# Queries turned three steps ahead through GpSimd, the minimum first on VectorE, and four weight chunks prepared in the first layer instead of in attention

## The chip, the cores and the metric

One core of a Trainium2 chip runs the whole program. The metric is the device time in microseconds (us). The kernel before was timed three times: 667.3, 667.43 and 668.02 us, median 667.43 us.

## The reference

The input is attention with a local window and block summaries (2 batches, 8 heads, 768 positions, head size 64), followed by two gated layers on 1536 tokens (512 to 2048 to 512). Cut to what is computed:

```
k_sum = max of k over blocks of 32;  v_sum = mean of v over blocks of 32
s_l = q k^T / 8, only where |i - j| < 16;  s_s = q k_sum^T / 8 + log(32)
a = softmax([s_l, s_s]);  x = a [v; v_sum]          (heads side by side: 1536 x 512)
h = x w1_in;  x = (h cos h) w1_out                  (layer 1)
h = x w2_in;  out = (h tanh(softplus h)) w2_out     (layer 2)
```

## The kernel before, in words

**Attention** (`attention`, lines 198 to 521) works on pairs of heads: 8 pairs, each cut into 3 chunks of 256 positions, so 24 steps `i = 3n + c` (pair `n`, chunk `c`). The loop at line 507 runs a software pipeline over these steps. In iteration `i` it does the scores of step `i` (`scores`: a mask product and four 128x118 products into bank `i % 2`, a minimum over each row on VectorE, four exponentials on ScalarE with row sums; the scores are negated, so the minimum stands for the maximum), the reciprocal and scaling of step `i - 1` (`softmax`, reciprocal on VectorE, product on GpSimd), the transposes of the probabilities of step `i - 2` (`probsT`, copied to SBUF by ScalarE as `pt`), the product with the values of step `i - 3` (`pv`), and the split of the result of step `i - 4` into a high part `xh` (ScalarE) and a low part `xl` (VectorE) in `evac`.

Beside these, the table `PREP` (lines 376 to 408) says in which iteration the inputs of later pairs are loaded and prepared. `prep_k` turns 256 columns of keys with TensorE, copies them into `KX` on ScalarE and takes block maxima on VectorE; `prep_ks` spreads the maxima into gaps of `KX` on GpSimd. `prep_q` turns queries and writes them into the block-diagonal `QB`, with two 64x256 VectorE operations for each chunk, one iteration before the scores that read it. `prep_vm` makes block means of the values with 24 products, and `prep_vs` copies them into `VW` by DMAs issued from SyncE (SP); for later pairs the block sums come from GpSimd (`load_vb`, `block_sums`). There is one tile `vb`, so the second `load_vb` (planned for iteration 7) waits until GpSimd has written the sums `vs` of the first (iteration 8), and the loads planned behind it wait with it on SP's queue.

Nothing reorders the instructions: `at` collects those of one iteration by phase and `flush` emits them phase by phase in the order of `ORDER` (line 262), so each engine gets its work in exactly that order. Before the change the order on VectorE is `xl` (step `i - 4`), minimum (step `i`), reciprocal (step `i - 1`), query writes, key maxima. On ScalarE it is `xh`, `pt`, exponentials, key copy. After `flush` comes `filler(i)`, which emits what `AT` holds for iteration `i`.

**Weights** are 64-bit floats in memory. A chunk of 128x512 is loaded (`wload`), narrowed to 32 bits in four parts (`wnarrow`: one on ScalarE at line 131, three on VectorE at lines 135, 138 and 141), and split into a high part (ScalarE, line 149) and a low part (line 152, on GpSimd for the first group, else on VectorE). The first group of layer 1 has 8 chunks: chunks 0 to 3 of `w1_in`, 4 to 7 of `w1_out`. Before the change `AT` spreads all eight over iterations 1 to 23 of attention. In the layers, `WSEQ` gives the same work for later groups, by tile number.

**Layer 1** (`layers`, the loop at line 623) takes 48 tiles `k`. `up(k)` is 12 products into bank `k % 4` (2.7 us at full clock). VectorE and ScalarE then make the gate: `turns(k)` (two VectorE operations, lines 551 and 552), in the next iteration `cos_gate` (sine on ScalarE, line 558 on VectorE) and `split` (line 544). After `split` come the operations of `WSEQ[k]`. `down` is 12 products that take four tiles of gates and chunks 4 to 7 of the group, one chunk for each three products. The first `down` stands after `up(6)`. `up(0)` to `up(2)` run inside the last iterations of attention. `up(k + 4)` needs the bank that `cos_gate(k)` has read. Layer 2 has its own order and isn't touched.

Of the kernel before, what the change touches and what calls it, by code (L numbers as in the profile page):

```python
# [21 lines left out]
def kernel(  # L22
# [122 lines left out]
    def wsplit(l, g, c, part=None):  # L145
        x = wstage[l, g, c]
        hi, lo = wdst(l, g, c)
        if part != 1:
            nc.scalar.copy(hi, x)  # L149
        if part != 0:  # L150
            eng = nc.gpsimd if (l, g) == (0, 0) else nc.vector
            eng.tensor_tensor(out=lo, in0=x, in1=hi.bitcast(F32), op=ALU.subtract)
# [45 lines left out]
    def attention(filler):  # L198
        with ExitStack() as es:
# [61 lines left out]

            ORDER = ("xh", "xl", "sc", "max", "rec", "norm", "tp", "pth", "exp", "tr", "ev", "kmax", "pv", "misc")
            todo = {o: [] for o in ORDER}

# [78 lines left out]
            def prep_ks(n):  # L343

                ks = KS.pop(n)
                x = KX[n % 2][:, HALO:HALO + NSUB * PITCH].rearrange("d (t w) -> d t w", w=PITCH)
                for h in range(2):
                    at("misc", nc.gpsimd.tensor_copy, x[:, h:NSUB:2, 0:GAP],
                       ks[:, None, GAP * h:GAP * h + GAP].to_broadcast([128, NSUB // 2, GAP]))
                at("misc", nc.gpsimd.tensor_copy, KX[n % 2][:, HALO + NSUB * PITCH:HALO + NSUB * PITCH + GAP],  # L350
                   ks[:, 0:GAP])
# [13 lines left out]
            def prep_q(n, c, bank=5):  # L365
                ps = turned(n, "q", c, bank).rearrange("d (s j) -> d s j", s=4)
                for e in range(2):
                    r = slice(64 * e, 64 * e + 64)
                    dst = QB[n % 2][r, 4 * c:4 * c + 4, e, :]
                    if n:  # L370
                        at("ev", nc.vector.tensor_scalar, out=dst, in0=ps[r], scalar1=-1.0 / SQD, scalar2=None,
                           op0=ALU.mult)
                    else:
                        at("ev", nc.scalar.activation, out=dst, in_=ps[r], func=AF.Copy, scale=-1.0 / SQD)
# [7 lines left out]
            for i, fn, n, c, bank in (  # L382
                (0, prep_q, 0, 1, 5), (1, prep_q, 0, 2, 5), (1, prep_k, 1, 0, 4), (2, prep_k, 1, 1, 4),
                (2, prep_k, 1, 2, 6), (2, prep_q, 1, 0, 5), (2, prep_q, 1, 1, 7), (3, prep_q, 1, 2, 5),
                (3, prep_k, 2, 0, 4), (3, prep_k, 2, 1, 7), (4, prep_k, 2, 2, 4),
            ):
                plan(i, fn, n, c, bank)
            plan(0, prep_vm, 0)
            plan(1, prep_vs, 0)
            plan(0, load_v, 1)  # L390
            plan(1, load_v, 2)
            for n in range(2, NP):
                plan({2: 0, 3: 3}.get(n, 3 * n - 7), load, n, "k")
                plan(max(3 * n - 4, 2), load, n, "q")
                for c in range(NCK):
                    if n > 2:
                        plan(3 * n - 4 + c, prep_k, n, c)
                    plan(3 * n - 1 + c, prep_q, n, c)
            for n in range(1, NP):
# [15 lines left out]
            def scores(i):  # L415
# [4 lines left out]
                SM[i] = sm  # L420
                if i < 2:
                    warm(2 * WARM_STEP, 2 + i)
                at("sc", nc.tensor.matmul, ps, lhsT=msel.rearrange("p e j -> p (e j)"), rhs=mask[:, c:c + 4, :],
# [72 lines left out]
            build_means()  # L496
            nc.gpsimd.memset(VW[1], 0.0)
            nc.gpsimd.memset(VW[2], 0.0)
            warm(1, 5)
            warm(WARM - 1, 3)  # L500
            for f in (lambda: prep_k(0, 0, 4), lambda: prep_k(0, 1, 6), lambda: prep_k(0, 2, 7),
                      lambda: prep_q(0, 0, 5)):
                f()
                flush()
                warm(1, 3)
            blank(QB[1])
            for i in range(NS + 5):
                if i >= 4 and i - 4 < NS:
                    evac(i - 4)
                if i < NS:  # L510
                    scores(i)
                if 1 <= i < NS + 1:
                    softmax(i - 1)
                if 2 <= i < NS + 2:
                    probsT(i - 2)
                for f in PREP.get(i, ()):
                    f()
                if 3 <= i < NS + 3:
                    pv(i - 3)
                flush()  # L520
                filler(i)
# [351 lines left out]
    def wseq(k, fn, *a):  # L873
        WSEQ.setdefault(k, []).append(lambda: fn(*a))

    for x in range(NG):
        chunks = [(0, x + 1, c) for c in range(NCH)]
        if x == NG - 1:
            chunks = [(1, 0, c) for c in range(HC)] + [(1, 1, 2), (1, 1, 3)]
        for c, w in enumerate(chunks):  # L880
            t0 = GF * NBLK * x + (2 if x == 0 else 0) + 3 * c // 2
            wseq(t0, wload, *w)
# [9 lines left out]

    for c in range(NCH):
        t0 = 5 * c + 3
        at_step(t0 // 2, wload, 0, 0, c)
        for part in range(4):
            at_step((t0 + 7 + part) // 2, wnarrow, 0, 0, c, part)
        at_step((t0 + 11) // 2, wsplit, 0, 0, c)

# [38 lines left out]
```

## Time and profile before

| | |
|---|---|
| median of 3 runs | 667.43 us |
| the profiled execution, its own time | 666.38 us |
| its span | 664.3 us |
| TensorE busy | 616.5 us (93%) |
| VectorE busy | 508.1 us (76%) |
| ScalarE busy | 334.7 us (50%) |
| GpSimd busy | 76.3 us (11%) |

The span is what the trace covers; 2.1 us of the profiled execution lie around it. All starts in the rows are counted from the beginning of the span. Rows of line 266 are those of attention, since `flush` emits them all; the tile names (`mx` the minimum, `pb` the exponentials, `rs` the reciprocal, `pn` the scaled probabilities, `pt` their transposes, `qb` the queries, `kx` the keys, `ks` the block maxima) tell them apart. Engines: PE is TensorE, DVE is VectorE, ACT is ScalarE, POOL is GpSimd, SPq is SyncE's queue.

### The profile page before, as it was taken

How to read it: one execution, taken by the hardware profiler on the slowest of the kernel's cores; microseconds unless marked ns; L12 is line 12 of the kernel's file. 1: busy time of each engine (PE TensorE's matmuls, PEld its weight loads, DVE VectorE, ACT ScalarE, POOL GpSimd, SP SyncE). 2: the span in 40 equal slices, each digit the busy share in tenths (PEclk: the TensorE clock that was granted, in tenths of full speed). 3: DMA queues.
4: the chain of work that ended last, by engine and by line, in shares of the span. 5: the costliest groups of instructions: out<-in, count | busy, mean ns of one | idle time of the engine just before them, and what ended most of it. 6: DMA issues, size and time to landing. Idle time of an engine off the chain costs nothing.

```text
span 664.3 us, 8374 instructions
## 1 busy us (share of the span) xinstructions
PE 616.5 (93%) x2962; PEld 515.0 (78%) x2962; DVE 508.1 (76%) x893; ACT 334.7 (50%) x730; POOL 76.3 (11%) x125
## 2 busy tenths in 40 slices
PE   7784677679999999999999999999999999999998
PEld 4674567568888888888888888888888888888886
DVE  3375376766987988888888995977788888898653
ACT  3465457656765644444444555655353434444230
POOL 6244254330000000000000223000000000000000
PEclk9797797889999999999999999999999999999999
DMA  9965486420122312122111210131212111221004
GB/s 176 180 137 120 89 166 143 88 65 0 64 95 65 95 64 64 64 64 63 64 64 65 64 63 1 32 97 32 96 33 95 61 66 64 64 85 43 0 17 174
DMA packets 61207, 51.17 MB, mean 77 GB/s; under 512 B 48158, under 2 KB 49278, under 8 KB 60926
## 3 DMA queue, kind: packets, MB, share of 16 engines
q1 hardware_dynamic: 61166, 50.65, 29.0%
q8 instruction: 23, 0.38, 0.2%
q14 instruction: 18, 0.15, 0.1%
HBM read 46.31 MB, written 3.15 MB: 74 GB/s over the span
## 4 chain that ended last, share of the span: by engine, by line
PE 86%; DVE 6%; ACT 4%; POOL 1%; SPq 1%; issue 1%; DMA 0%; ACTq 0%; POOLq 0%
PE bank L188 20%; PE bank L703 20%; PE bank L574 20%; PE bank L688 18%; PE bank L266 9%; ACT pb L266 2%; DVE mx L266 2%; DVE xl L266 2%; DVE qb L266 1%; SPq L279 1%; ACT xh L266 1%; DVE rs L266 0%; SPq L266 0%; DMA vw<-vm 0%; ACT kx L266 0%
## 5 line engine op out<-in xcount | busy, mean ns | idle before, releaser
L188 PE MATMUL bank<-xh,ws 128*128 128x512 f32 x384 | 126.7, 393 | 0.0
L574 PE MATMUL bank<-gh,ws 128*128 128x512 f32 x384 | 125.4, 389 | 0.0
L703 PE MATMUL bank<-ws,gh 128*128 128x512 f32 (+1 forms) x388 | 118.4, 387 | 0.0
L688 PE MATMUL bank<-xh,ws 128*128 128x512 f32 x272 | 91.0, 389 | 0.0
L188 PEld LDWEIGHTS bank<-xh,ws 128*128 128x128 f32 x384 | 72.8, 190 | 15.2
L703 PEld LDWEIGHTS bank<-ws,gh 128*128 128x128 f32 x388 | 72.7, 188 | 14.9
L574 PEld LDWEIGHTS bank<-gh,ws 128*128 128x128 f32 x384 | 72.1, 188 | 15.0
L188 PE MATMUL bank<-xl,ws 128*128 128x512 f32 x192 | 75.2, 392 | 0.0
L703 PE MATMUL bank<-ws,gl 128*128 128x512 f32 (+1 forms) x194 | 75.0, 387 | 0.0
L574 PE MATMUL bank<-gl,ws 128*128 128x512 f32 x192 | 74.7, 389 | 0.0
L550 ACT ACTIVATE n<-bank,b_quarter 128x512 int32<-128x512 f32 x48 | 33.0, 687 | 79.9 <-PE bank L188 79.9
L149 ACT CAST ws<-wx 128x512 fp32r<-128x512 f32 x64 | 39.7, 622 | 56.5 <-DVE wx L141 56.5
L266 PE MATMUL bank<-kx,qb 128*128 128x118 f32 x192 | 32.1, 320 | 29.5 <-DVE qb L266 22.0
L688 PEld LDWEIGHTS bank<-xh,ws 128*128 128x128 f32 x272 | 51.1, 188 | 10.5
L659 DVE TENSOR_TENSOR gl<-gg,gh 128x512 fp32r<-128x512 f32 x48 | 34.0, 707 | 30.3 <-ACT gh L658 30.3
L266 PEld LDWEIGHTS bank<-kx,qb 128*128 128x128 f32 x192 | 28.8, 226 | 36.3 <-DVE qb L266 16.3
L715 DVE TENSOR_TENSOR acc<-acc,bank 128x512 f32<-128x512 f32 (+1 forms) x71 | 47.4, 674 | 8.5 <-PE bank L703 8.4
L688 PE MATMUL bank<-xl,ws 128*128 128x512 f32 x136 | 52.9, 389 | 0.0
L551 DVE SCALAR_TENSOR_TENSOR r<-n,bank 128x512 f32<-128x512 int32 x48 | 32.9, 685 | 23.1 <-ACT n L550 23.0
L138 DVE SCALAR_TENSOR_TENSOR wx<-wst,wx 128x512 int32<-128x512 int32 x64 | 46.3, 723 | 2.1
L266 ACT ACTIVATE pb<-bank,mx 128x118 f32<-128x118 f32 x96 | 33.2, 360 | 26.6 <-DVE mx L266 25.5
L141 DVE SCALAR_TENSOR_TENSOR wx<-wst,wx 128x512 int32<-128x512 int32 x64 | 44.1, 690 | 1.6
(107 smaller groups left out, 1039.7 us busy)
## 6 DMA issues: line engine op xcount, KB each, us to landing
wst<-in_moe_w_in_dram SPq DMA_DIRECT2D x32, 512.0 KB
wst<-in_moe_w_out_dram SPq DMA_DIRECT2D x32, 512.0 KB
kn<-in_k_dram SPq DMA_DIRECT2D x16, 192.0 KB
qn<-in_q_dram SPq DMA_DIRECT2D x16, 192.0 KB
vw<-in_v_dram SPq DMA_DIRECT2D x16, 192.0 KB
out_dram<-acc SPq DMA_DIRECT2D x11, 256.0 KB
vb<-in_v_dram SPq DMA_DIRECT2D x2, 960.0 KB
vw<-in_v_dram SPq DMA_DIRECT2D x32, 41.2 KB
```

Of the source, the lines that this page charges most:

```text
L138: nc.vector.scalar_tensor_tensor(out=xi, in0=word[:, :, 0], scalar=29, in1=xi, op0=ALU.logical_shift_right, op1=ALU.bitwise_or)
L141: nc.vector.scalar_tensor_tensor(out=xi, in0=word[:, :, 1], scalar=-2 ** 31, in1=xi, op0=ALU.bitwise_and, op1=ALU.bitwise_or)
L149: nc.scalar.copy(hi, x)
L188: nc.tensor.matmul(ps, lhsT=SLOT[4 * (g % 2) + a][:, 512 * c + 128 * f:512 * c + 128 * f + 128], rhs=X[e][:, c, TB * j:TB * j + TB], start ...
L266: todo[phase].append(lambda: fn(*a, **kw))
L550: nc.scalar.activation(out=n, in_=h, func=AF.Identity, scale=1.0 / TWO_PI, bias=b_quarter)
L551: nc.vector.scalar_tensor_tensor(out=r, in0=n, scalar=-C1, in1=h, op0=ALU.mult, op1=ALU.add)
L574: nc.tensor.matmul(ps, lhsT=x, rhs=y, start=(n == 0), stop=(n == len(mm) - 1))
L659: later.append(lambda: nc.vector.tensor_tensor(out=lo, in0=g, in1=hi.bitcast(F32), op=ALU.subtract))
L688: nc.tensor.matmul(ps, lhsT=u, rhs=v, start=start and n == 0, stop=stop and n == len(mm) - 1)
L703: nc.tensor.matmul(ps, lhsT=x, rhs=y, start=(n == 0 and (h == 0 or not stay)), stop=(n == len(mm) - 1 and (h == NH - 1 or not stay)))
L715: nc.vector.tensor_tensor(out=acc, in0=acc, in1=ps, op=ALU.add)
```

## The change

Queries: each chunk of pairs 1 to 7 is copied out of PSUM by one 128x256 VectorE operation into a new tile `qt` and written into `QB` by two GpSimd copies, three iterations before the scores that read it; the query loads are planned two iterations earlier. All three query chunks of pair 0 are turned before the loop. The spreading of the first pair's key maxima goes to VectorE, and the clearing of `VW[1]` and `VW[2]` behind the preparation of pair 0. The order within an iteration changes on every engine, and `softmax` works on step `i` in iteration `i`. Of the first group's weight chunks only 0 to 3 are narrowed in attention (iterations 10 to 19). Chunks 4 and 5 are loaded there, and chunks 4 to 7 are narrowed and split in tiles 0 to 5 of layer 1, their low parts on VectorE. The first chunks of the second group are planned some tiles later. The number of products that only keep TensorE busy (`warm`) goes from two iterations to four.

```
-            eng = nc.gpsimd if (l, g) == (0, 0) else nc.vector
+            eng = nc.gpsimd if (l, g) == (0, 0) and c < KD else nc.vector
...
-            ORDER = ("xh", "xl", "sc", "max", "rec", "norm", "tp", "pth", "exp", "tr", "ev", "kmax", "pv", "misc")
+            ORDER = ("sc", "max", "exp", "tp", "tr", "qev", "rec", "norm", "xh", "xl", "ev", "pth", "kmax", "pv", "qbd", "misc")
...
+                eng = nc.gpsimd if n else nc.vector
                 for h in range(2):
-                    at("misc", nc.gpsimd.tensor_copy, x[:, h:NSUB:2, 0:GAP],
+                    at("misc", eng.tensor_copy, x[:, h:NSUB:2, 0:GAP],
...
+                ps = turned(n, "q", c, bank)
+                if n:
+                    qt = p2.tile([128, 256], F32, tag="qt", name="qt")
+                    at("qev", nc.vector.tensor_scalar, out=qt, in0=ps, scalar1=-1.0 / SQD, scalar2=None, op0=ALU.mult)
...
                     if n:
-                        at("ev", nc.vector.tensor_scalar, out=dst, in0=ps[r], scalar1=-1.0 / SQD, scalar2=None,
-                           op0=ALU.mult)
+                        at("qbd", nc.gpsimd.tensor_copy, dst, qt[r].rearrange("d (s j) -> d s j", s=4))
...
-                (0, prep_q, 0, 1, 5), (1, prep_q, 0, 2, 5), (1, prep_k, 1, 0, 4), (2, prep_k, 1, 1, 4),
-                (2, prep_k, 1, 2, 6), (2, prep_q, 1, 0, 5), (2, prep_q, 1, 1, 7), (3, prep_q, 1, 2, 5),
-                (3, prep_k, 2, 0, 4), (3, prep_k, 2, 1, 7), (4, prep_k, 2, 2, 4),
+                (1, prep_k, 1, 0, 4), (1, prep_k, 1, 1, 6), (1, prep_q, 1, 0, 5), (2, prep_k, 1, 2, 4),
+                (2, prep_q, 1, 1, 5), (2, prep_q, 1, 2, 7), (3, prep_k, 2, 0, 4), (3, prep_k, 2, 1, 7),
+                (4, prep_k, 2, 2, 4),
...
-                plan(max(3 * n - 4, 2), load, n, "q")
+                plan(3 * n - 6, load, n, "q")
...
-                    plan(3 * n - 1 + c, prep_q, n, c)
+                    plan(3 * n - 3 + c, prep_q, n, c)
...
-                if i < 2:
-                    warm(2 * WARM_STEP, 2 + i)
+                if i < 4:
+                    warm(2 * WARM_STEP, i % 2)
...
             blank(QB[1])
+            nc.gpsimd.memset(VW[1], 0.0)
+            nc.gpsimd.memset(VW[2], 0.0)
...
                     scores(i)
-                if 1 <= i < NS + 1:
-                    softmax(i - 1)
+                    softmax(i)
...
+    for c in range(KD, NCH):
+        t0 = c - KD + (c - KD) // 2
+        if c >= KD + 2:
+            wseq(t0 - 2, wload, 0, 0, c)
+        for part in range(4):
+            wseq(t0, wnarrow, 0, 0, c, part)
+        wseq(t0 + 1, wsplit, 0, 0, c)
...
-            t0 = GF * NBLK * x + (2 if x == 0 else 0) + 3 * c // 2
+            t0 = GF * NBLK * x + (3 * c // 2 if x else 4 + 4 * c // 3)
...
-    for c in range(NCH):
-        t0 = 5 * c + 3
-        at_step(t0 // 2, wload, 0, 0, c)
+    for c, (t0, t1) in enumerate(((7, 10), (9, 12), (12, 15), (14, 17))):
+        at_step(t0, wload, 0, 0, c)
         for part in range(4):
-            at_step((t0 + 7 + part) // 2, wnarrow, 0, 0, c, part)
-        at_step((t0 + 11) // 2, wsplit, 0, 0, c)
+            at_step(t1 + part // 2, wnarrow, 0, 0, c, part)
+        at_step(t1 + 2, wsplit, 0, 0, c)
+    at_step(17, wload, 0, 0, 4)
+    at_step(19, wload, 0, 0, 5)
```

## Rows read from the trace of the kernel before

**Rows 1.** Busy time by stretch, start of layer 1: stretch, length, PE, PEld, DVE, ACT, POOL, PEclk, DMA

```profile
153.60:172.30 18.70, 18.70 (x84) 15.45 (x83) 16.17 (x27) 13.59 (x22) 0.00 (x0) 1.00 0.05 11
```

**Rows 2.** Chain that ended last, attention, two turns: start us, us, what

```profile
118.20 2.93 PE bank L266 x24
...
123.35 0.28 ACT kx L266
...
126.90 0.66 DVE mx L266
...
127.65 1.47 ACT pb L266 x8
129.12 0.56 ACT wx L131
...
130.33 0.42 DVE xl L266
...
131.22 0.65 DVE mx L266
```

**Rows 3.** Timeline of VectorE, the minima of steps 8, 10 and 23

```profile
55.34 0.65 DVE L266 TENSOR_REDUCE mx<-bank 128x4 f32<-128x472 f32 x1
...
75.18 0.65 DVE L266 TENSOR_REDUCE mx<-bank 128x4 f32<-128x472 f32 x1 [0.45 <-PE bank L266]
...
140.48 0.65 DVE L266 TENSOR_REDUCE mx<-bank 128x4 f32<-128x472 f32 x1
```

**Rows 4.** VectorE by line and shape, 75.1 to 140.4 us: busy us, mean ns | idle before

```profile
L266 DVE TENSOR_REDUCE ks<-bank 128x8 f32<-128x256 f32 x10 | 4.2, 425 | 7.6 <-ACT kx L266 7.6
L138 DVE SCALAR_TENSOR_TENSOR wx<-wst,wx 128x512 int32<-128x512 int32 x5 | 4.2, 844 | 0.1
```

**Rows 5.** Timelines of SP and PE around the long wait of iteration 9

```profile
58.29 0.34 SPq L299 DMA_DIRECT2D vb<-in_v_dram  x1
...
65.42 3.88 SPq L266 DMA_DIRECT2D vw<-vm  x4
...
71.01 2.05 PE L266 MATMUL bank<-pt,vw 118*128 118x128 f32 x8 [10.98 <-DMA vw<-vm]
```

**Rows 6.** GpSimd by line and shape, then a collision in the timeline

```profile
L266 POOL TENSOR_TENSOR vb<-vb 120x256 f32<-120x256 f32 x14 | 9.9, 725 | 0.0
L266 POOL COPY kx<-ks 128x72 f32<-128x72 f32 x16 | 4.8, 305 | 6.2 <-DVE ks L266 3.5 <-ACT kx L266 2.7
...
141.71 0.97 POOL L266 TENSOR_TENSOR pn<-pb,rs 128x472 f32<-128x472 f32 x1 [2.01 <-DVE rs L266]
...
141.89 1.34 DVE L138 SCALAR_TENSOR_TENSOR wx<-wst,wx 128x512 int32<-128x512 int32 x1
```

**Rows 7.** Timelines of DVE and PE in the first tiles of layer 1

```profile
155.33 0.69 DVE L551 SCALAR_TENSOR_TENSOR r<-n,bank 128x512 f32<-128x512 int32 x1
...
165.96 0.69 DVE L558 TENSOR_TENSOR gg<-r,bank 128x512 f32<-128x512 f32 x1 [0.19 <-ACT r L556]
...
167.10 0.39 PE L574 MATMUL bank<-gh,ws 128*128 128x512 f32 x1
...
168.50 0.42 DVE L135 TENSOR_SCALAR wx<-wx 128x512 int32<-128x512 int32 x1
...
169.82 0.39 PE L188 MATMUL bank<-xh,ws 128*128 128x512 f32 x1
...
170.29 0.68 DVE L558 TENSOR_TENSOR gg<-r,bank 128x512 f32<-128x512 f32 x1
...
172.81 0.69 DVE L152 TENSOR_TENSOR ws<-wx,ws 128x512 fp32r<-128x512 f32 x1
173.41 0.42 DVE L135 TENSOR_SCALAR wx<-wx 128x512 int32<-128x512 int32 x1
```

**Rows 8.** Chain that ended last, the first two `up` tiles of layer 1

```profile
144.70 3.96 PE bank L188 x12
...
149.99 2.74 PE bank L188 x12
```

More of the change, by code (lines that the diff above doesn't have):

```diff
@@ L346, in prep_ks @@
                 x = KX[n % 2][:, HALO:HALO + NSUB * PITCH].rearrange("d (t w) -> d t w", w=PITCH)
+                eng = nc.gpsimd if n else nc.vector
                 for h in range(2):
-                    at("misc", nc.gpsimd.tensor_copy, x[:, h:NSUB:2, 0:GAP],
+                    at("misc", eng.tensor_copy, x[:, h:NSUB:2, 0:GAP],
                        ks[:, None, GAP * h:GAP * h + GAP].to_broadcast([128, NSUB // 2, GAP]))
-                at("misc", nc.gpsimd.tensor_copy, KX[n % 2][:, HALO + NSUB * PITCH:HALO + NSUB * PITCH + GAP],
+                at("misc", eng.tensor_copy, KX[n % 2][:, HALO + NSUB * PITCH:HALO + NSUB * PITCH + GAP],
                    ks[:, 0:GAP])
@@ L365, in prep_q @@
             def prep_q(n, c, bank=5):
-                ps = turned(n, "q", c, bank).rearrange("d (s j) -> d s j", s=4)
+                ps = turned(n, "q", c, bank)
+                if n:
+                    qt = p2.tile([128, 256], F32, tag="qt", name="qt")
+                    at("qev", nc.vector.tensor_scalar, out=qt, in0=ps, scalar1=-1.0 / SQD, scalar2=None, op0=ALU.mult)
+                ps = ps.rearrange("d (s j) -> d s j", s=4)
                 for e in range(2):
@@ L389, in attention @@
             plan(1, prep_vs, 0)
-            plan(0, load_v, 1)
-            plan(1, load_v, 2)
             for n in range(2, NP):
                 plan({2: 0, 3: 3}.get(n, 3 * n - 7), load, n, "k")
-                plan(max(3 * n - 4, 2), load, n, "q")
+                plan(3 * n - 6, load, n, "q")
                 for c in range(NCK):
@@ L397, in attention @@
                         plan(3 * n - 4 + c, prep_k, n, c)
-                    plan(3 * n - 1 + c, prep_q, n, c)
+                    plan(3 * n - 3 + c, prep_q, n, c)
+            plan(0, load_v, 1)
+            plan(1, load_v, 2)
             for n in range(1, NP):
@@ L496, in attention @@
             build_means()
-            nc.gpsimd.memset(VW[1], 0.0)
-            nc.gpsimd.memset(VW[2], 0.0)
             warm(1, 5)
@@ L501, in attention @@
             for f in (lambda: prep_k(0, 0, 4), lambda: prep_k(0, 1, 6), lambda: prep_k(0, 2, 7),
-                      lambda: prep_q(0, 0, 5)):
+                      lambda: prep_q(0, 0, 5), lambda: prep_q(0, 1, 4), lambda: prep_q(0, 2, 6)):
                 f()
```

## The prediction

> **What bounds the kernel now.** I read the slices of the span first, then busy time by stretch, the chain of waits, and the timelines of the two places that the change touches. Two stages have different limits.
>
> From the end of attention on, TensorE is the bound: in the first 18.7 us of layer 1 it is busy for 18.7 us [rows 1]. Whatever makes TensorE wait there is added to the time. VectorE is nearly full in the same stretch, 16.17 of 18.70 us, so it has little room for more.
>
> In attention TensorE idles, and the chain goes round between VectorE and ScalarE. One turn [rows 2]: the minimum at 126.90, exponentials from 127.65, then the first narrowing of a weight chunk (0.56), then `xh`, `xl`, and the next minimum at 131.22. That is 4.32 us, 3.76 without the weight. Steps that also copy keys put 0.28 more into the chain, 4.04 in all. From the minimum of step 10 to that of step 23 there are 13 turns in 65.3 us [rows 3], 5.02 each; 13 turns of 4.04 would be 52.5, and the weight chunks make most of the other 12.8. VectorE's part of the narrowing is mostly hidden in this order: it stands between the key maxima and `xl`, where VectorE waits for the exponentials and `xh` anyway.
>
> A third place is one wait of 10.98 us in iteration 9: the product with the values waits for block means that come by DMA [rows 5]. Their issue stands on SP's queue behind the second `vb` load, which starts only when GpSimd has finished the first sums.
>
> **The change, part by part.** The sum is made against the profiled execution (span 664.3, own time 666.38 us, 1.05 below the median 667.43).
>
> *1. Queries and order: the turn.* The query write by VectorE one iteration ahead goes; TensorE no longer waits for it. But TensorE is not what closes most turns; where it stands in the chain (2.93 from 118.20 [rows 2]), VectorE's own queue ends within 0.1 us of it. In the new order VectorE has minimum, query copy, reciprocal of the same step, `xl`, key maximum, weights. The reciprocal must wait for this step's exponentials, and what is queued behind it on VectorE waits too: `xl`, the key maximum, the weights, and the next minimum. The new turn is then minimum, exponentials, `xh`, `xl` as before (3.76), plus the key maximum, 0.42 [rows 4], which now stands between `xl` and the next minimum: 4.18. The key copy leaves the chain, since ScalarE does it beside `xl`. The query copy and reciprocal cost nothing, covered by the wait for exponentials and `xh`; if that cover went, they would cost about 0.8. GpSimd's two new copies are bounded by 0.31 (72 columns) and 0.73 (an addition of 256 columns) [rows 6]; I take 0.48 each, nearer the copy. Their result is needed three steps later, so they delay only what is behind them on GpSimd.
>
> *2. Weights in attention.* Now VectorE's narrowing stands directly before the next minimum, with no wait to hide in. One chunk is 1.79 undisturbed (168.50 to 170.29 [rows 7]), plus 0.15 for meeting GpSimd (line 138 takes 844 ns on average here [rows 4] against 0.69 for an operation of that form in the layers [rows 7]), plus about 0.55 of waiting for ScalarE's first part, which is emitted behind the exponentials, `xh` and the copies: 2.5. Bounds: 1.5 and 3.2. Four chunks stand in iterations 10 to 19: 10.0. Of the 13 turns, ten with the key maximum give 41.8, three without 11.3. Sum 63.1 against 65.3: **2.2 us gained** (8 gained to 1 lost).
>
> A row shows the meeting: the product of GpSimd starts at 141.71 and ends at 142.68; line 138, started at 141.89, takes 1.34 and ends 0.55 after that, as if it had begun then [rows 6].
>
> The Trainium skill (SBUF — State Buffer, Who interferes with whom) has a rule for it that speaks against this change: VectorE with two SBUF inputs and a GpSimd instruction that reads SBUF shut each other out for a whole instruction, whoever came first. The trace agrees; by it each chunk would wait out a GpSimd copy, about 0.5 in place of 0.15, and the result would be some 1.4 us later than mine.
>
> *3. Up to step 10.* The scores of step 0 no longer wait for GpSimd's clearing, all queries of pair 0 are ready, and two chunks leave iterations 5 to 9; the steps that make means stay bound by TensorE. I take the minimum of step 8 as 2.7 us earlier than 55.34 [rows 3] (bounds 1 and 5). The long wait stays, because `load_vb` is not touched. GpSimd finished the sums just before SP's `vb` issue at 58.29, 2.9 after that minimum [rows 3, 5]. In the new order it first scales step 8, which waits for that step's exponentials (0.75 + 1.47 + 0.4), needs 0.97 itself, then does the two query copies (0.96) and the last two small sums (about 0.35 each, by the small copy [rows 6]): with the handovers 5.4. From the `vb` issue to the product took 12.7 (58.29 to 71.01). On SP one weight load takes the place of two query loads, with fewer packets but no fewer bytes, so SP is blocked less and the DMA engines as long; I take 11.5 (bounds 9 and 13). So the wait ends 16.9 after the minimum in place of 15.7, and of 2.7 us **1.5 are left** (4 gained to 0.5 lost).
>
> *4. Drain.* At the end the product of step 21 waits for `pt`, now last on ScalarE, some 3.5 after the last minimum (0.75 + 1.35 until the exponentials let it go on, `xh` 0.75, `pt` about 0.6); with the product `up(0)` is on the chain some 4.6 after that minimum, now 4.2 [rows 3, 8]: **0.4 later** (0 to 0.8). Loads: the query loads move by two iterations and past the value loads; SP has nothing else to do then, nothing is late.
>
> *5. Layer 1.* The first `down` runs from 167.10 to 169.82; its last product, which needs the low part of chunk 7, starts at 169.6 [rows 7]. VectorE starts layer 1 at 155.33. One tile of gate costs it 2.54 (165.96 to 168.50), the narrowing of a chunk 1.79, a low part 0.60 (172.81 to 173.41). Before that low part stand now: two operations of tile 0 (1.3), five tiles (12.7), four chunks narrowed (7.2) and four low parts (2.4): 23.6, which ends at 178.9 on this clock. TensorE can't go round it: `up(3)` to `up(6)` have their banks and are over before that, and after `up(6)` comes this `down`. It waits **9.4 us**. Bounds 8 and 11. After such a wait it doesn't run at full clock at once: the first `up` after the drain took 3.96, the second 2.74 [rows 8]; **1.2 more**. Later tiles cost VectorE at most 4.9 against 5.4 of TensorE's, so nothing is caught up and nothing more is lost. The later plan for the second group costs nothing: its chunk 3 is done some 2 us before `up(12)` needs it.
>
> The sum: -2.2 - 1.5 + 0.4 + 9.4 + 1.2 = +7.3, so 673.7 for the profiled execution and **674.7** against the median.
>
> **The rivals.** *The turn gets shorter than its chain (faster).* If VectorE and ScalarE overlap more than I see (`xl` starting on the first half of `xh`, the reciprocal not holding up what is behind it), TensorE's own work could set the turn: 2.93 for 24 products of a step [rows 2], with the mask some 3.2. Place: the 13 turns from step 10. Price: at 3.2 in place of 4.18 and 3.76 some 11.5 us, which gives 663. It decides from a turn of 3.6 downwards, where my 7.3 are eaten up. For it: the change takes 0.4 of VectorE's work out of a step and TensorE loses its waits. Against: the turn from 126.90 to 131.22 closes without TensorE, and the reciprocal's wait is in the new order itself.
>
> *GpSimd gets in the way (slower still).* Scaling (0.97), two copies (0.96), two block sums (1.45) [rows 6] and a low part fall together in iterations 12 and 14, about a turn's length. If each narrowing waits for whole instructions and the key gaps come late, 3 to 6 us are added: 678 to 681.
>
> *The weights only change place (no change).* If narrowing a chunk costs attention as much as the start of layer 1, and the four chunks removed gave back all 10 us there, the result would be 667.4. For it: 12.8 us over 13 turns is over 2 us for each chunk now. Against: the four that stay lose their cover.
>
> **How the numbers follow.** The forecast has 0.62 (669 to 679), the slower rival 0.14, the faster one 0.16, no change 0.08. About 0.2% (1.3 us) is what a measurement of this kernel can tell from no change. The ends of all terms together reach from 664 to 682; 666 to 681 leaves out most of the faster rival's far side and little above.
>
> **What would show it.** Right: turns of 4.2 without weights; a wait of about 11 us for the means in iteration 9; the first `down` waiting 9 to 10 us for VectorE's low part of chunk 7, with TensorE below full clock behind it; TensorE without waits from then on. Wrong: turns under 3.6, the wait for the means gone, or a first `down` that starts as soon after `up(6)` as now.

## The result, and the profile after

The kernel after takes **677.29 us** (median of 4 runs, 674.55 to 679.88); the kernel before took 667.72 beside it. The ratio is 1.0142, 95% interval 1.0101 to 1.0183: slower, as forecast, by 9.6 us where 7.3 were predicted. The profiled execution after is the lowest of its four runs, 674.55 with a span of 672.6, against a span of 664.3 before: 8.3 us longer. The accounting below is of these two spans.

The profile's busy times of the kernel after (us, share of the span, instructions):

```profile
PE 621.8 (92%) x2971; PEld 517.9 (77%) x2972; DVE 503.1 (75%) x879; ACT 333.7 (50%) x730; POOL 87.0 (13%) x160
```

VectorE lost 5.0 us of work and GpSimd gained 10.7 (76.3 before). Neither number tells that the time grew; for that the stretches must be set side by side. The minima of steps 8, 10, 22 and 23 in VectorE's timeline after answer to [rows 3] (start us, us, engine, line, operation, tiles, shapes, and in brackets the idle time before it and its releaser):

```profile
50.99 0.65 DVE L266 TENSOR_REDUCE mx<-bank 128x4 f32<-128x472 f32 x1 [1.20 <-PE bank L266]
...
72.56 0.65 DVE L266 TENSOR_REDUCE mx<-bank 128x4 f32<-128x472 f32 x1 [13.29 <-PE bank L266]
...
132.91 0.65 DVE L266 TENSOR_REDUCE mx<-bank 128x4 f32<-128x472 f32 x1
136.67 0.65 DVE L266 TENSOR_REDUCE mx<-bank 128x4 f32<-128x472 f32 x1
```

Attention ends earlier. The last two turns, with no key maximum and no weights, take 3.76 each. The turn from step 19 to step 20 (minima at 121.11 and 125.21), with a key maximum, takes 4.10.

In layer 1 the gain is lost. TensorE's timeline after, around the first `down` (line 577 is line 574 of before), answers to [rows 7]:

```profile
161.44 0.50 PE L188 MATMUL bank<-xh,ws 128*128 128x512 f32 x1 [1.91 <-DVE gg L561]
...
168.66 0.39 PE L577 MATMUL bank<-gh,ws 128*128 128x512 f32 x1
...
171.41 0.50 PE L577 MATMUL bank<-gh,ws 128*128 128x512 f32 x1 [0.62 <-DVE ws L152]
174.97 0.50 PE L577 MATMUL bank<-gh,ws 128*128 128x512 f32 x1 [3.06 <-ACT ws L149]
...
176.32 0.80 PE L577 MATMUL bank<-gh,ws 128*128 128x512 f32 x1 [0.62 <-DVE ws L152]
176.91 0.63 PE L188 MATMUL bank<-xh,ws 128*128 128x512 f32 x1
```

VectorE's timeline after, its first operation of tile 0 and the low part of chunk 7, also to [rows 7]:

```profile
152.67 0.69 DVE L554 SCALAR_TENSOR_TENSOR r<-n,bank 128x512 f32<-128x512 int32 x1
...
175.58 0.68 DVE L152 TENSOR_TENSOR ws<-wx,ws 128x512 fp32r<-128x512 f32 x1
```

The last product of the first `down` starts 0.06 after that low part has ended. The wait of 3.06 in the middle is for the high part of chunk 7, which ScalarE makes at 174.30; it stands there behind line 546, which had waited 2.02 for VectorE (line 561). So this wait too goes back to VectorE's queue. The row at 161.44 is the first product of `up(5)`: TensorE already waits there, 1.91 for the gate of tile 1. From tile 0 on VectorE to `up(7)` on TensorE are 24.24 us (152.67 to 176.91); before they were 14.49. The chain of waits after, `up(0)` and then the two pieces behind the wait of the first `down`, answers to [rows 8]:

```profile
141.63 4.36 PE bank L188 x12
...
177.12 3.85 PE bank L188 x12
180.97 2.73 PE bank L577 x12
```

Where the 8.3 us of span come from:

| stretch | before | after | difference | predicted |
|---|---|---|---|---|
| start to minimum of step 10 | 75.18 | 72.56 | -2.6 | -1.5 |
| minimum 10 to minimum 23 | 65.30 | 64.11 | -1.2 | -2.2 |
| minimum 23 to tile 0 on VectorE | 14.85 | 16.00 | +1.15 | +0.4 |
| tile 0 on VectorE to `up(7)` | 14.49 | 24.24 | +9.75 | +9.4 |
| `up(7)`, lower clock (12 products at full clock: 2.73) | 2.73 | 3.85 | +1.1 | +1.2 |
| sum | | | +8.2 | +7.3 |

Two more places were named in the prediction. The long wait of iteration 9, timelines of SP and TensorE after, to [rows 5]:

```profile
56.45 0.34 SPq L299 DMA_DIRECT2D vb<-in_v_dram  x1
...
58.80 4.92 SPq L266 DMA_DIRECT2D vw<-vm  x4
...
68.39 2.05 PE L266 MATMUL bank<-pt,vw 118*128 118x128 f32 x8 [12.72 <-DMA vw<-in_v_dram]
```

The `vb` issue stands 5.46 after the minimum of step 8, and the product goes on 17.4 after it (predicted 5.4 and 16.9). The wait is still there. What the profile names as its end is a load of values now (`in_v_dram`), before it was the copies of the means (`vm`); both stand behind the `vb` issue on SP's queue. Next, VectorE's groups between the minima of steps 10 and 23 (busy us, mean ns | idle before), to [rows 4]:

```profile
L138 DVE SCALAR_TENSOR_TENSOR wx<-wst,wx 128x512 int32<-128x512 int32 x4 | 3.6, 893 | 0.1
L141 DVE SCALAR_TENSOR_TENSOR wx<-wst,wx 128x512 int32<-128x512 int32 x4 | 3.2, 794 | 0.1
L135 DVE TENSOR_SCALAR wx<-wx 128x512 int32<-128x512 int32 x4 | 3.1, 779 | 1.6 <-ACT wx L131 1.3
```

Undisturbed the three take 0.69, 0.69 and 0.42. Here one chunk needs 0.89 + 0.79 + 0.78 = 2.46, and its share of the waiting in front of line 135 is 0.4.

### The profile page after: what moved, and what is told of

The parts are those of the page before. It is cut to its first block, busy times and chain, and to the rows that moved or that the text cites. A ratio compares the mean times of both kernels' runs of the same rounds, so it can differ in the third digit from the quotient of the medians.

```text
span 672.6 us, 8404 instructions
## 1 busy us (share of the span) xinstructions
PE 621.8 (92%) x2971; PEld 517.9 (77%) x2972; DVE 503.1 (75%) x879; ACT 333.7 (50%) x730; POOL 87.0 (13%) x160
## 4 chain that ended last, share of the span: by engine, by line
PE 79%; ACT 7%; DVE 7%; POOL 2%; issue 2%; DMA 1%; SPq 0%; ACTq 0%; POOLq 0%; DVEq 0%
PE bank L706 19%; PE bank L577 19%; PE bank L691 18%; PE bank L188 18%; PE bank L266 5%; ACT pb L266 4%; DVE mx L266 2%; ACT xh L266 1%; DMA kn<-in_k_dram 1%; DVE wx L138 1%; ACT pt L266 1%; ACT kx L266 1%; DVE r L555 1%; DVE r L554 1%; DVE ks L266 1%
## 5 line engine op out<-in xcount | busy, mean ns | idle before, releaser
L188 PE MATMUL bank<-xh,ws 128*128 128x512 f32 x384 | 129.4, 399 | 2.0 <-DVE gg L561 1.9
L691 PE MATMUL bank<-xh,ws 128*128 128x512 f32 x272 | 91.0, 389 | 0.0
L188 PEld LDWEIGHTS bank<-xh,ws 128*128 128x128 f32 x384 | 74.4, 194 | 18.5 <-DVE gg L561 2.8
L188 PE MATMUL bank<-xl,ws 128*128 128x512 f32 x192 | 76.6, 399 | 0.0
L149 ACT CAST ws<-wx 128x512 fp32r<-128x512 f32 x64 | 39.6, 620 | 51.5 <-DVE wx L141 51.5
L691 PEld LDWEIGHTS bank<-xh,ws 128*128 128x128 f32 x272 | 51.1, 188 | 10.6
L691 PE MATMUL bank<-xl,ws 128*128 128x512 f32 x136 | 52.9, 389 | 0.0
L592 POOL TENSOR_TENSOR xl<-acc,xh 128x512 fp32r<-128x512 f32 x10 | 14.6, 1474 | 263.1 <-ACT xh L590 263.1
L266 PE MATMUL bank<-pt,vw 118*128 118x128 f32 x192 | 30.0, 306 | 18.3 <-DMA vw<-in_v_dram 12.7
```

The source lines that it names most:

```text
L188: nc.tensor.matmul(ps, lhsT=SLOT[4 * (g % 2) + a][:, 512 * c + 128 * f:512 * c + 128 * f + 128], rhs=X[e][:, c, TB * j:TB * j + TB], start ...
L266: todo[phase].append(lambda: fn(*a, **kw))
L691: nc.tensor.matmul(ps, lhsT=u, rhs=v, start=start and n == 0, stop=stop and n == len(mm) - 1)
```

## The experiments

Ratios are to the kernel before, measured beside each run on the same chip; its medians in those runs lie between 667.04 and 667.57. My theory after the result: the four chunks left to layer 1 cost 10.9 there, and attention gives only a few us of it back. The main rival: the new order and the queries are what costs.

### The change cut in two

**e1**: the kernel after with the weights of before, the plan of the second group's first chunks with them.

```
-            eng = nc.gpsimd if (l, g) == (0, 0) and c < KD else nc.vector
+            eng = nc.gpsimd if (l, g) == (0, 0) else nc.vector
...
-    for c in range(KD, NCH):
-        t0 = c - KD + (c - KD) // 2
...
-    for c, (t0, t1) in enumerate(((7, 10), (9, 12), (12, 15), (14, 17))):
...
+    for c in range(NCH):
+        t0 = 5 * c + 3
+        at_step(t0 // 2, wload, 0, 0, c)
         for part in range(4):
+            at_step((t0 + 7 + part) // 2, wnarrow, 0, 0, c, part)
+        at_step((t0 + 11) // 2, wsplit, 0, 0, c)
```

> The kernel after, with all eight chunks of the first group narrowed in attention again, by the table of before, low parts on GpSimd. Theory (the four chunks left to layer 1 cost 9.75 of waiting for the low part of chunk 7 and 1.1 of lower clock; a chunk in attention costs 2.5 to 3.0 where it stands in front of the minimum): the wait of the first down is gone, -10.9; four more chunks in attention, of which about two fall before the wait for the means and cost nothing there, so +6 to +12. From 677.3 that is 672 to 678. Rival (the new order hides narrowing, only the place in layer 1 costs): 665 to 668. Second rival (the new order itself is what is slow): 677 or more with no wait in layer 1 and plain turns over 4.5.

Measured: 666.73 us, ratio 1.0007 (0.9993 to 1.0021). **No difference from before.** The queries and the order, without the move of the weights, are worth nothing in sum. The wait in layer 1 is gone, as the theory says, but the result is 5 us under its range: I had priced a chunk of attention at 2.5 to 3.0 from the table of after. Between the minima of steps 10 and 23 of e1 lie 64.68 us (73.68 to 138.36) and five chunks. Ten turns of 4.10 and three of 3.76 are 52.3, so a chunk costs 2.5 here; in the kernel after 64.11 less 52.3 is 11.8 for four, 2.95 each. The same work, spread otherwise, meets GpSimd and ScalarE's first part less often: the three operations take 2.21 for a chunk in place of 2.46 (line 141 alone is longer, 853 ns), and the waiting in front of line 135 is 0.1 in place of 0.4. The other two groups of VectorE in e1, in the window from 73 to 140 us:

```profile
L138 DVE SCALAR_TENSOR_TENSOR wx<-wst,wx 128x512 int32<-128x512 int32 x5 | 3.9, 787 | 0.2
L135 DVE TENSOR_SCALAR wx<-wx 128x512 int32<-128x512 int32 x5 | 2.9, 571 | 0.6 <-ACT wx L131 0.3
```

The gain of the new order ahead of the last minimum (138.36 against 140.48) is given back behind it: tile 0 of layer 1 starts on VectorE at 155.63, before at 155.33.

**e2**: the kernel before with the weights of after, the same edit the other way round.

```
-            eng = nc.gpsimd if (l, g) == (0, 0) else nc.vector
+            eng = nc.gpsimd if (l, g) == (0, 0) and c < KD else nc.vector
...
+    for c in range(KD, NCH):
+        t0 = c - KD + (c - KD) // 2
...
+    for c, (t0, t1) in enumerate(((7, 10), (9, 12), (12, 15), (14, 17))):
```

> The kernel before, its queries and its order untouched, with only the change to the weights: chunks 0 to 3 in iterations 10 to 19, chunks 4 to 7 in tiles 0 to 5 of layer 1. Theory: layer 1 loses the same 10.9 as in the kernel after; attention gains about 2 for each of the chunks that leave steps 10 to 23 (two of the six there) and 1 to 2 before the wait for the means: 667.7 + 10.9 - 4 - 2 = about 673, between 670 and 676. Rival (the loss comes from the new order, and VectorE's order of before would also hide the weights in layer 1): 665 to 668.

Measured: 674.13 us, ratio 1.0113 (1.0087 to 1.0139): the theory's number within 1.2 us, the rival is out. The weights alone make most of the loss, 7.1 of some 9.6. The 3.2 between the medians of e2 and of the kernel after are not explained by the traces: the two profiled executions have the same span, 672.6. TensorE's timeline of e2 shows the same last wait as after:

```profile
174.18 0.80 PE L574 MATMUL bank<-gh,ws 128*128 128x512 f32 x1 [3.06 <-ACT ws L149]
```

Turns without weights are 4.02 in the order of before (54.81 to 58.83) and 4.10 in that of after (the prediction had 4.04 and 4.18), so the new order makes no turn shorter. One thing here was not expected: with no weights in the drain, the order of before needs 13.25 from the last minimum (138.63) to tile 0 on VectorE (151.88), the new one 16.00. The chain of waits of e2 in the drain:

```profile
139.87 0.98 POOL pn L266
...
140.90 1.55 PE bank L266 x12
142.44 2.77 PE bank L188 x12
```

Here `up(0)` takes 2.77 and starts 3.81 after the last minimum; in the kernel after it takes 4.36 and starts 4.96 after it (141.63 less 136.67). These two, 1.6 and 1.15, are the whole 2.75. The granted clock of just that stretch in the kernel after (stretch, length, busy us and count of PE, PEld, DVE, ACT, POOL, then PEclk, DMA share, GB/s), followed by those of the wait in the first `down` and of `up(7)`:

```profile
141.63:145.99 4.36, 4.36 (x15) 3.35 (x14) 0.86 (x3) 0.73 (x2) 0.00 (x0) 0.61 0.01 4
...
168.66:176.32 7.66, 3.36 (x12) 1.72 (x10) 7.52 (x14) 5.26 (x9) 0.00 (x0) 0.97 0.44 137
177.12:180.97 3.85, 3.85 (x13) 3.08 (x13) 3.75 (x7) 2.18 (x4) 0.00 (x0) 0.71 0.00 0
```

0.61 and 0.71 are means over stretches in which the clock goes from its lower level, 1.2 GHz, to the upper, 2.4 GHz. Both stand behind waits of TensorE (2.15 in front of the product ahead of `up(0)`, 4.3 in all in the first `down`), and the stretch with the waits of the `down` is itself granted nearly the full clock (0.97): the price is paid in the work after it. Not every wait has this price: in e2 TensorE waits 1.68 in front of the transposes at 140.90, and its `up(0)` runs in 2.77, the length at full clock. What decides between the two isn't shown.

### The price of a chunk in layer 1

**e7**: only chunks 6 and 7 left to layer 1.

```
-    for c in range(KD, NCH):
+    for c in range(KD + 2, NCH):
...
-    for c, (t0, t1) in enumerate(((7, 10), (9, 12), (12, 15), (14, 17))):
+    for c, (t0, t1) in enumerate(((7, 10), (9, 12), (12, 15), (14, 17), (17, 20), (19, 22))):
...
-    at_step(17, wload, 0, 0, 4)
-    at_step(19, wload, 0, 0, 5)
```

> The kernel after, with chunks 4 and 5 also narrowed in attention (iterations 20 to 24, low parts on GpSimd), so that only chunks 6 and 7 are left to layer 1. Theory (the wait of the first down is VectorE's queue, 1.79 + 0.60 for each chunk before the low part of chunk 7): the wait falls by 4.8, from 9.8 to about 5, with the lower clock behind it still there; attention gives back 2 x 2 to 3 = 4 to 6; the result stays at 677.3 within 1.5. Rival (the wait is not a sum over chunks but a late load or ScalarE's part): wait unchanged, 681 or more.

Measured: 675.64 us, ratio 1.0131 (1.0109 to 1.0152). VectorE and TensorE in the timelines of e7, tile 0 and the waits of the first `down`:

```profile
159.19 0.69 DVE L554 SCALAR_TENSOR_TENSOR r<-n,bank 128x512 f32<-128x512 int32 x1
...
161.40 0.69 DVE L561 TENSOR_TENSOR gg<-r,bank 128x512 f32<-128x512 f32 x1 [0.79 <-ACT r L559]
...
174.58 0.50 PE L577 MATMUL bank<-gh,ws 128*128 128x512 f32 x1 [0.62 <-DVE ws L152]
178.14 0.79 PE L577 MATMUL bank<-gh,ws 128*128 128x512 f32 x1 [3.06 <-ACT ws L149]
...
179.49 0.80 PE L577 MATMUL bank<-gh,ws 128*128 128x512 f32 x1
```

The last product of the first `down` starts 20.30 after tile 0 (after: 23.65, 176.32 less 152.67): 3.35 less for two chunks, where 4.8 were expected. The wait does shrink with the number of chunks, so it is VectorE's queue. Only 3.35 of the 4.8 of work taken out came back, because chunks 6 and 7 kept their places in tiles 3 to 5: with nothing else to do in tiles 0 to 2, VectorE waits there for ScalarE's sine, 0.79 and twice 0.19, which is 1.17 of the missing 1.4. In attention the two chunks took 3.87 between the minima of steps 10 and 23 (74.22 to 142.20, 67.98 for 64.11) and 0.99 in the drain (16.99 for 16.00), 2.4 each; in layer 1 a chunk was worth 1.7 here. In the traces e7 should lose 1.5 by this, and its median is 1.65 under that of the kernel after, whose runs spread over 5.3: which place is the dearer is not settled. One more thing follows from e7. Up to step 10 its program is that of the kernel after, and yet its minima of steps 8 and 10 stand at 52.73 and 74.22, there at 50.99 and 72.56:

```profile
74.22 0.65 DVE L266 TENSOR_REDUCE mx<-bank 128x4 f32<-128x472 f32 x1 [13.21 <-PE bank L266]
```

So differences of up to 1.7 in the first stretch lie within what two executions of one program show.

### What a chunk costs in attention, and why

**e5**: VectorE's three parts of each chunk between the query copy and the reciprocal.

```
-            ORDER = ("sc", "max", "exp", "tp", "tr", "qev", "rec",
+            ORDER = ("sc", "max", "exp", "tp", "tr", "qev", "fill", "rec",
...
         at_step(t0, wload, 0, 0, c)
-        for part in range(4):
-            at_step(t1 + part // 2, wnarrow, 0, 0, c, part)
+        at_step(t1, wnarrow, 0, 0, c, 0)
+        for part in range(1, 4):
+            FILL.setdefault(t1 + 1 + part // 2, []).append(lambda c=c, part=part: wnarrow(0, 0, c, part))
...
+                for f in FILL.get(i, ()):
+                    at("fill", f)
                 flush()
```

> The kernel after, with VectorE's three parts of the narrowing of the four attention chunks moved from behind the key maximum to between the query copy and the reciprocal, where VectorE waits about 1.3 for the exponentials; one or two parts in an iteration. Theory (the weights cost because they stand in front of the next minimum with nothing to hide in): of the 11.8 that four chunks cost between the minima of steps 10 and 23 some 7 to 9 go, 677.3 - 8 = 669, between 667 and 671. Rival (collisions with GpSimd and ScalarE's first part set the price, wherever the parts stand): 674 to 677.

Measured: 669.61 us, ratio 1.0045 (1.0026 to 1.0063), as the theory has it: 7.7 under the kernel after. VectorE's timeline of e5, the minima of steps 16 to 19:

```profile
98.01 0.64 DVE L266 TENSOR_REDUCE mx<-bank 128x4 f32<-128x472 f32 x1
102.09 0.64 DVE L266 TENSOR_REDUCE mx<-bank 128x4 f32<-128x472 f32 x1
106.18 0.64 DVE L266 TENSOR_REDUCE mx<-bank 128x4 f32<-128x472 f32 x1
115.18 0.65 DVE L266 TENSOR_REDUCE mx<-bank 128x4 f32<-128x472 f32 x1 [4.83 <-PE bank L266]
```

Turns that carry a chunk are 4.08 to 4.09, the length of a turn without one, but for one of 4.68 (step 12 to 13) and that of the wait below: in the wait for the exponentials narrowing costs almost nothing. From step 10 to 23 the turns take 57.74 where 52.3 would be all without weights; 4.9 of the rest is one new wait in front of step 19. TensorE stands there at the product with the values; the copies of the means of that pair, planned for iteration 15 (minimum at 93.92), were issued by SP from 102.72 to 109.46, since each pair's eight take it 6.6 to 7.5, and the product goes on at 111.01. The profile names no releaser for this wait. By time and program, what is late next, once VectorE is faster, is SP's queue.

**e9**: VectorE's key maximum in front of the reciprocal.

```
-            ORDER = ("sc", "max", "exp", "tp", "tr", "qev", "rec", "norm", "xh", "xl", "ev", "pth", "kmax", "pv", "qbd", "misc")
+            ORDER = ("sc", "max", "exp", "tp", "tr", "qev", "kmax", "rec", "norm", "xh", "xl", "ev", "pth", "pv", "qbd", "misc")
```

> The kernel after, with only VectorE's key maximum moved in front of the reciprocal, into the wait for the exponentials. Theory (the turn is minimum, exponentials, xh, xl plus the key maximum): turns with a key maximum and no weights fall from 4.10 to about 3.7, 13 steps from 10 to 23 give 10 x 0.4 = 4, and steps before the wait for the means give 1 to 2 that this wait mostly follows: 677.3 - 5 = 672, between 670 and 674. Rival (GpSimd, TensorE or ScalarE sets the turn of 4.10): turns stay at 4.0 to 4.1 and the time at 676 to 678.

Measured: 673.7 us, ratio 1.0105 (1.0078 to 1.0133), inside the theory's range by its median. The turn from step 8 to step 9, with a key maximum and no weights, takes 3.76 (53.05 to 56.81) in place of 4.10: the turn is the chain minimum, exponentials, `xh`, `xl`, plus whatever stands between `xl` and the next minimum. But the 13 turns gain only 1.2 (62.88 against 64.11), not the 4 expected: in turns with a chunk ScalarE's first part now comes later than VectorE wants it. VectorE's group of line 135 in e9, in the window from 72 to 140 us:

```profile
L135 DVE TENSOR_SCALAR wx<-wx 128x512 int32<-128x512 int32 x4 | 3.1, 768 | 3.2 <-ACT wx L131 3.2
```

**e6**: queries written by VectorE straight from PSUM, GpSimd's copies gone.

```
                 ps = turned(n, "q", c, bank)
-                if n:
-                    qt = p2.tile([128, 256], F32, tag="qt", name="qt")
-                    at("qev", nc.vector.tensor_scalar, out=qt, in0=ps, scalar1=-1.0 / SQD, scalar2=None, op0=ALU.mult)
...
-                        at("qbd", nc.gpsimd.tensor_copy, dst, qt[r].rearrange("d (s j) -> d s j", s=4))
+                        at("qev", nc.vector.tensor_scalar, out=dst, in0=ps[r], scalar1=-1.0 / SQD, scalar2=None, op0=ALU.mult)
```

> The kernel after, with the queries written into the block-diagonal tile straight from PSUM by VectorE, two operations of 64x256 at 0.42 each in place of one copy of 0.41 and two GpSimd copies; all else, the three iterations ahead included, stays. Theory (VectorE's extra 0.42 lies in the wait of 1.27 for the exponentials; GpSimd's copies stand behind the scaling and only collide with the narrowing): 677.3 less 0 to 2.5, that is 675 to 677. Rival (the GpSimd copies are what makes VectorE's order pay): 680 or more.

Measured: 671.13 us, ratio 1.0063 (1.004 to 1.0086): 6.2 under the kernel after, more than expected. **GpSimd's copies, which I had costed at next to nothing, cost 6 us.** The traces (span 668.2 against 672.6) show three places. Ahead of step 3, GpSimd in the kernel after has four query copies to make before it spreads the first key maxima of pair 1, and the scores wait for that. The timeline after, GpSimd and TensorE:

```profile
23.38 1.74 POOL L266 COPY qb<-qt 64x256 f32<-64x256 f32 x4
25.17 0.55 POOL L266 COPY kx<-ks 128x72 f32<-128x72 f32 x3
25.65 2.03 PE L266 MATMUL bank<-kx,qb 128*128 128x118 f32 x8 [4.18 <-POOL kx L266]
```

In e6 the wait is 2.48, the products take 1.15 (granted clock 1.00, in the kernel after 0.52), and they end 1.25 earlier:

```profile
24.80 0.55 POOL L266 COPY kx<-ks 128x72 f32<-128x72 f32 x3
...
25.28 1.15 PE L266 MATMUL bank<-kx,qb 128*128 128x118 f32 x8 [2.48 <-POOL kx L266]
```

By step 8 the lead is 2.0 (two executions of one program can differ by 1.7 here, as e7 shows; but the slowest run of e6, 672.19, is under the fastest of the kernel after, 674.55). The block sums, and with them the `vb` issue, come earlier: 0.7 off the long wait (72.56 - 50.99 = 21.57 after, 69.84 - 48.97 = 20.87 in e6). The other 1.3 are collisions: lines 135 and 138 take 636 and 735 ns on average in e6, 779 and 893 in the kernel after.

A collision in the timeline of the kernel after, to [rows 6]:

```profile
113.90 1.27 POOL L152 TENSOR_TENSOR ws<-wx,ws 128x512 fp32r<-128x512 f32 x1
114.11 1.34 DVE L135 TENSOR_SCALAR wx<-wx 128x512 int32<-128x512 int32 x1 [0.67 <-ACT wx L131]
```

Line 135 takes 0.42 alone. Here it started 0.21 after GpSimd's low part and ended 0.28 after it, as if it had waited for nearly the whole of it. The prediction's rule of the Trainium skill (SBUF — State Buffer, Who interferes with whom) covers this too: by it a `tensor_scalar` in a two-port mode and a GpSimd instruction shut each other out for a whole instruction. The trace agrees; that line 135 runs in such a mode, no run here shows. By that rule the prediction put the result 1.4 later than its own sum; the term it concerns, the 13 turns, came out 1.0 later.

### The wait of iteration 9, and what is to be had

**e3**: the kernel after with the second `vb` load two iterations later.

```
-                plan((2, 7)[g], load_vb, g)
+                plan((2, 9)[g], load_vb, g)
                 for c in range(9):
-                    plan((4, 10)[g] + c // 2, block_sums, g, c)
+                    plan((4 + c // 2, 11 + c // 3)[g], block_sums, g, c)
```

> The kernel after, with the second vb load planned for iteration 9 instead of 7 and its sums from iteration 11, three in an iteration, so that the loads of values and keys and the copies of the means no longer stand behind it on SP's queue. Theory: the wait of iteration 9 (12.7 in the after trace) shrinks to under 3, 677.3 - 10 = 667, between 664 and 670. Rival (the wait belongs to the transfers themselves, or the next pair's means or keys are late in its place): 672 to 678.

Measured: 663.35 us, ratio 0.9955 (0.9939 to 0.9971): 13.9 under the kernel after and **faster than before**. SP's timeline and VectorE's in e3:

```profile
49.55 3.46 SPq L266 DMA_DIRECT2D vw<-vm  x4
...
59.07 0.36 SPq L299 DMA_DIRECT2D vb<-in_v_dram  x1
```

```profile
55.28 0.64 DVE L266 TENSOR_REDUCE mx<-bank 128x4 f32<-128x472 f32 x1
59.37 0.64 DVE L266 TENSOR_REDUCE mx<-bank 128x4 f32<-128x472 f32 x1
```

The copies of the means are issued at 49.55 in place of 58.80, and step 10 follows step 9 after 4.09 in place of 17.47. Nothing takes the wait's place. It was a matter of the order on one queue.

**e8a**: e3, with all eight chunks in attention and VectorE's parts in the wait for the exponentials.

```
+    for c, t1 in enumerate((4, 6, 9, 11, 14, 16, 19, 21)):
+        at_step(t1 - 3, wload, 0, 0, c)
+        at_step(t1, wnarrow, 0, 0, c, 0)
+        for part in range(1, 4):
+            FILL.setdefault(t1 + 1 + part // 2, []).append(lambda c=c, part=part: wnarrow(0, 0, c, part))
+        at_step(t1 + 2, wsplit, 0, 0, c)
```

> The kernel after, with the second vb load in iteration 9 and its sums from 11 as in e3, and all eight chunks narrowed in attention, VectorE's parts in the wait for the exponentials as in e5, none left to layer 1. Theory (the three costs add: the wait for the means 13.9, narrowing in front of the minimum, the chunks in layer 1): from the 663.4 of e3 another 10.9 in layer 1 and 5 to 10 in attention, 643 to 650. Rival (SP's queue, which needs some 15 to 17 for one pair's loads and copies of means, becomes the bound of attention): a wait for means or weights of 5 or more in each later pair, 653 to 662.

Measured: 649.09 us, ratio 0.9717 (0.9692 to 0.9743). The costs add, as the theory says. The rival is there in part: one turn takes 8.10.

**e8b**: e8a with the queries of e6 and the value loads one iteration later.

```
-                    plan(3 * n - 3, load_v, n)
+                    plan(3 * n - 2, load_v, n)
```

> The kernel of e8a, with the queries written straight from PSUM by VectorE as in e6, and the value loads of pairs 3 to 7 issued one iteration later, behind the copies of the means on SP's queue instead of ahead of them. Theory (what is left over 4.1 in e8a's turns is SP's queue, 8.10 in place of 4.09 at one step, and GpSimd's collisions): 649.1 less 3 to 5 for the means less 2 to 4 for GpSimd, 640 to 645. Rival (SP's total per pair is the bound, whatever the order; VectorE's wait for the exponentials is full): 647 to 650.

Measured: **642.8 us, ratio 0.9648 (0.9623 to 0.9672)**, the best of all: 24.5 under the kernel before beside it, 34 under the kernel after. No turn from step 10 on is longer than 4.99 now; ahead of it the turns to steps 7 and 8 have grown to 7.46 and 6.12 (in e8a 4.37 and 5.52). The two edits were not run apart here.

**e8c**: e8b with the value loads on ScalarE's queue.

```
+                dma = (nc.scalar if n > 2 else nc.sync).dma_start
...
-                    nc.sync.dma_start(out=x[SIDE:SIDE + SUB, :, e, :], in_=src)
+                    dma(out=x[SIDE:SIDE + SUB, :, e, :], in_=src)
```

> The kernel of e8b, with the six value loads of each of pairs 3 to 7 issued by ScalarE instead of SP. Theory (SP's queue is a bound of these pairs, and an issue costs ScalarE little, since it waits for the minimum): 1 to 4 below e8b. Rival (an issue holds ScalarE as long as it shows on SP, 0.4 to 0.7, 4 for each pair, in front of the exponentials): 5 to 15 above e8b.

Measured: 664.12 us, ratio 0.9963 (0.9941 to 0.9985), 21 above e8b: the rival's sign, and more than its price. ScalarE's queue and ScalarE in the timeline of e8c:

```profile
66.58 0.61 ACTq L289 DMA_DIRECT2D vw<-in_v_dram  x1
...
68.49 0.36 ACT L266 ACTIVATE pb<-bank,mx 128x118 f32<-128x118 f32 x1 [7.03 <-DMA vw<-in_v_dram]
```

The issues themselves are about 0.6 each. What costs is that they wait, and the exponentials of step 10 wait behind them: their minimum was done at 61.92, and ScalarE idles for 7.03 us in front of them. Four waits with such a load as their releaser sum to 20.7 in this run; a fifth, of 8.05, ends with a copy of the means (`vs`). What held the issues until 66.58 is not shown: the earlier transfers into the same tile are the likely cause, and that was only argued.

## Why the prediction was right, and where its steps failed

The sign and the largest term held. **Layer 1** (*step 5*): the low part of chunk 7 was put 23.6 behind the start of tile 0 and ended 23.6 behind it; the stretch grew by 9.75 for 9.4, the lower clock behind it came to 1.1 for 1.2. e1 takes both away and e7 shrinks the wait. One sentence of the step failed: that `up(3)` to `up(6)` "have their banks". `up(5)` waited 1.91 for the gate of tile 1, the 24 products from there on took 7.22 in place of 5.46 (twice 2.73; granted clock 0.60 in the first 4.22 us), and the first `down` starts 15.99 behind tile 0, before 11.77. So not all of the 9.4 is waiting in the `down`; TensorE's waits in this stretch sum to 6.2. It changed nothing in the sum, since the low part on VectorE sets the end. Behind `up(7)` both kernels need the same, 491.6 to the end of the span. This one term, worked out from durations of the kernel before, is what decided the case.

**Steps 10 to 23** (*step 2*): 1.2 gained where 2.2 were predicted. The plain turns were mis-sized by 0.8 in my favour (4.10 and 3.76 for 4.18 and 3.76; 52.3 for 53.1), the chunks by 1.8 against me (11.8 for 10.0). The part that failed is the 0.15 allowed for meeting GpSimd: the three operations took 0.66 over their undisturbed sum of 1.80. One sentence of the opening was wrong as well: that narrowing is mostly hidden in the order of before. Plain turns there are 4.02 (e2), so 13 turns would be 51.5, and the five chunks between steps 10 and 23 cost 13.8, 2.8 each, where VectorE's part alone is 1.8. ScalarE's timeline of before shows one reason, in the turn from 121.14 to 126.90: the chunk's high part waits for VectorE's last narrowing, and `xh` stands behind it.

```profile
124.71 0.62 ACT L149 CAST ws<-wx 128x512 fp32r<-128x512 f32 x1 [1.09 <-DVE wx L141]
```

So the narrowing had little cover in the order of before.

**Queries** (*step 1*): that GpSimd's two copies "delay only what is behind them on GpSimd" was right as a sentence and wrong as a price. What is behind them are the key spreads of pair 1, which TensorE waits for, and the block sums; what is beside them is VectorE's narrowing. I had put only the collisions (0.15 a chunk) and the later `vb` issue into the sum. e6 prices the copies at 6.2 in the median, 4.4 in the span.

**Up to step 10** (*step 3*): 2.6 gained for 1.5. The minimum of step 8 came 4.35 earlier, not 2.7; that the means would stay late behind it, and by how much (17.4 for 16.9), held. In e7, with the same program up to there, the two figures are 1.0 and 2.6, so the size is known to some 1.7 only. And that it came near the forecast is in part luck: without GpSimd's copies (e6) step 10 comes 5.3 earlier than before (69.84 for 75.18), so two misses, the gain put too low and the copies left out, stand against each other.

**Drain** (*step 4*): +1.15 for +0.4, above its bound of 0.8. The step counted the later `pt`, and by too little: `up(0)` is on the chain 4.96 after the last minimum, not 4.6 (before 4.22). It left out that `up(0)` itself could run slower than before: 4.36 for 3.96. The two make 0.74 and 0.40. Against e2, which has the same weights, the new order costs 2.75 in the drain; the 1.15 is what is left after the weights also went out of it (before the change, chunk 7 is narrowed in iterations 22 to 24).

Of the **rivals**, "the weights only change place" was near the mark in its statement, that a chunk costs attention about as much as layer 1 (e7: 4.9 for two in attention, the drain included). It failed because the chunks of before lay partly where nothing was to be gained: two of them before the wait of iteration 9, which swallows what is saved there (in e2, without those two, step 10 comes at 76.00, before at 75.18). "GpSimd in the way" named a cost that is real (e6), and larger than the forecast's share for it. The result still came out below its 678, by the median, in part because step 3 had put its own gain too low. "The turn gets shorter than its chain" is out: 4.10 in place of 4.02.

The median lies 2.6 above the forecast, the profiled execution 0.85 above its own (674.55 for 673.7). The misses in the table, -1.1, +1.0, +0.75, +0.35 and -0.1, cancel for the larger part, which is luck. The rest is the spread of the runs after, told of below.

## What to carry to other kernels

Work moved out of a stage with slack has to be priced in the queue that it joins: here fifteen more operations of VectorE in front of one low part became a wait of TensorE, plus a lower clock behind it. Before moving work, look for the wait of its own engine in the stage where it is: putting the same operations into the wait for the exponentials made them almost free (e5), and moving one load on one queue gave back more than the whole change had cost (e3). A copy handed to an idle engine isn't free if that engine's queue also feeds TensorE.

## What the runs showed that was not expected

- The same narrowing of a chunk costs attention 2.95, 2.5 or almost nothing (after, e1, e5), by its place among the other operations.
- The four runs of the kernel after spread over 5.3 us, those of before beside it over 1.0 (24 runs of before, beside the first four experiments: 3.5). The times after rise as the mean granted clock falls: 674.55 at 0.967, 676.9 at 0.965, 677.68 at 0.962, 679.88 at 0.960. What sets the clock apart from run to run, and whether it is the cause of the longer time or follows from it, stays open.
- A transfer issued from an engine that computes makes that engine wait in its order: 7.03 us in front of the exponentials (e8c), while the issue itself shows as 0.6.
